# Six levels of row counts instead of four for the experts of a fused attention, dense and routed MLP kernel

## The chip, the cores and the metric

The kernel runs on one core of one Trainium2 chip. The metric is the device time of one launch in microseconds (us). TensorE (PE), VectorE (DVE), ScalarE (ACT), GpSimd (POOL) and SyncE (SP) each work through their own instructions in order; SP issues nearly all DMAs.

## The reference, cut to what matters

Attention over 2 batches, 8 heads and 576 positions gives 1152 tokens of 512 features. A dense layer with the activation `h * cos(h)` follows, and then a routed layer of 8 experts:

```python
def _moe2_ref(x, w_gate, w1, w2, capacity):      # x 1152 x 512, w1 8 x 512 x 1024, w2 8 x 1024 x 512
    expert_idx = np.argmax(x @ w_gate, axis=1)
    ...
    for i in range(N):                            # each token goes to one expert, up to capacity 288
        e = expert_idx[i]
        if counts[e] < capacity:
            disp[e, counts[e]] = x[i]
    ...
    h = np.maximum(np.einsum('ecd,edf->ecf', disp, w1), 0.0)
    y = np.einsum('ecf,efd->ecd', h, w2)
    ...
            out[i] = gate_w[i] * y[expert_idx[i], pos[i]]
```

How many tokens an expert gets depends on the inputs. Counted with the reference on its default draw, experts 0 to 7 get 206, 162, 138, 155, 108, 127, 112 and 144.

## The kernel before, in words

One core does everything in stages: attention (to about 100 us), the first dense matmul (to 200 us), the second dense matmul with the routing (to 309 us), and the experts (from 295 us to the end). Every product is done in three fp16 matmuls (high by high, high by low, low by high), so each weight that comes from DRAM in float32 is split in two on the chip.

**Rows of an expert.** The tokens are scattered by expert into a DRAM buffer `disp` with room for 288 rows an expert. A matmul needs a row count that is fixed in the program, but the counts are known only at run time. So the kernel holds several whole programs for the experts, one for each line of a table SIZES (a level), and takes the first level whose eight row counts are all large enough; a general program with 288 rows each stands behind them. The choice is made in `counts()`: `limit` holds the counts of all levels (filled by POOL memsets of one element in `consts2`, L172), one DVE comparison a level is made (L1201), and a sum over them gives the number of levels that are too small. Every engine then branches on that number (`arms`, L1351).

**Which expert is which.** The two experts expected to be largest (expert 0, and one chosen after five of nine token tiles) have their first 144 rows worked ahead of the branch. The columns of SIZES are then: what those two have left over (columns 1 and 2), the whole of the third chosen expert (column 3), and the other five in order of size (columns 4 to 8). Below they are called experts A to H by column. With the counts above they need 62, 14, 162, 144, 138, 127, 112 and 108 rows.

**One expert of `ns` rows** (`expert`, L1032). Its rows come by a transposing DMA into `eX` (ns rounded up to 16 rows, L1011). Layer 1 is eight blocks of 128 hidden features, each 12 matmuls of `ns` columns into one PSUM bank (L1042), evicted by ACT (the high half, with ReLU, L1044) and DVE (the low half, L1045) into `eH`. Layer 2 has two forms:

```python
    def flipped(ns):
        return ns <= 112 or 128 < ns <= 224
```

Flipped: four blocks of 24 matmuls with `ns` columns (L1064), four evictions (L1066), eight transposes for more than 128 rows or four for fewer (L1071), then one or two scaled stores (L1050). Not flipped: 24 matmuls of 512 columns for each 128 rows (L1081), and the store. The stores go to POOL, which scatters the rows to the output (L1051); padding rows are dropped there.

**The weights.** An expert has eight loads of 512 KB (four of w1, four of w2), each into one of four staging tiles `ws` (SP, L967 and L971), which ACT (high half, L656) and DVE (low half, L657) split; then the tile is free for the next load. The pairs of buffers `win`, `gall`, `gall`, `wout` take the experts in turn: D and H use `wout`, E `win`, F and G `gall`. At the branch 40 loads are still to be split, those of D to H. They are numbered 1 to 40 here: 1 to 8 are D's, 25 to 28 G's w1, 29 to 32 G's w2, 33 to 36 H's w1, 37 to 40 H's w2.

**The order.** Within a level the work of an expert and the next are interleaved by `adv(e, k)`, which takes expert e up to its step k (LA is 4, LB is 4):

```python
        for e in range(n):
            ...
            adv(e, KE)                 # rest of layer 1
            state["l1"] = e + 1
            adv(e + 1, la)             # next expert: four blocks of layer 1
            ...
            adv(e, KE + l2s[e])        # layer 2
            adv(e + 1, lb)
            adv(e, KE + l2s[e] + 1)    # transposes, stores
```

How many splits are put between these steps is set by a credit that grows with the matmul columns written so far (in `adv`: `12 * ns` for a block of layer 1, `12 * cols` for a step of layer 2), and the scheduler of the framework then settles the order in which each engine's instructions stand. PSUM has six banks for this, `ps_s`, `ps_pt` and `ps_mm` with two each, taken in turn.

Of the kernel before, what the change touches and what calls it, by code (L numbers as in the profile page):

```python
# [39 lines left out]
NST = 1  # L40
HALF = 1
SIZES = (
# [4 lines left out]
)  # L47
WP = 8
XR = 4
# [1333 lines left out]
```

## Time and profile before

| | |
|---|---|
| time, median of 3 runs | 434.71 us (433.16 to 439.06) |
| the profiled execution's own time | 437.53 us |
| its span from first to last instruction | 435.8 us |
| share of the span busy: PE, DVE, ACT, POOL | 92%, 72%, 63%, 34% |
| mean clock of TensorE granted | 0.98 of full speed |
| first matmul behind the branch | 328.61 us |
| last matmul ends, last store of rows issued | 429.0, 430.05 us |

The profile is one execution on the chip. Times are microseconds from the start of the span, durations of an instruction count from its start to its end, and a busy PE is not PE at its peak, since matmuls overlap: what a row of matmuls costs is read from the start of the next one. "[2.59 <-DVE eH L1045]" behind a row is idle time ahead of it and what ended it. L12 is line 12 of the kernel before; in the kernel after, every line from the table on is two lines further down.

### The profile page before, as it was taken

The numbers are of one execution on the slowest core, as the hardware profiler recorded it, in microseconds if no ns is written. First come the engines' busy times: TensorE is split into PE (matmuls) and PEld (weight loads), VectorE is DVE, ScalarE is ACT, GpSimd is POOL, SyncE is SP. The second block draws the span as 40 slices with busy tenths as digits, with TensorE's granted clock in tenths as the row PEclk, the third lists the DMA queues.
The fourth block names the chain that finished last, engine by engine and source line by source line (L and its number), as shares of the span: only waits on it lengthen the run. The fifth ranks groups of instructions, "written<-read, shape, count | busy, mean of one in ns | idle before, by whom it ended". The sixth has DMA issues, their size and how long they took to land.

```text
span 435.8 us, 10790 instructions
## 1 busy us (share of the span) xinstructions
PE 401.6 (92%) x4008; PEld 291.5 (67%) x4008; DVE 312.6 (72%) x767; ACT 275.6 (63%) x634; POOL 150.0 (34%) x242
## 2 busy tenths in 40 slices
PE   2799999999999999989999999797999999798893
PEld 1588888886666666544444454355988999798862
DVE  7769999749998499989875665654824576667570
ACT  6679989977888577775234433525536667677560
POOL 7668888553454345445000032010011012022030
PEclk9989999999999999999999999899999999899898
DMA  7979995103389933312567476758697689888741
GB/s 164 206 169 195 165 214 142 52 2 99 97 231 304 335 121 99 96 57 90 193 186 236 111 160 225 221 127 252 206 213 159 178 277 251 312 280 278 250 133 39
DMA packets 91228, 77.61 MB, mean 178 GB/s; under 512 B 64006, under 2 KB 72198, under 8 KB 91167
## 3 DMA queue, kind: packets, MB, share of 16 engines
q1 hardware_dynamic: 87855, 71.85, 60.2%
q0 software_dynamic: 2256, 4.73, 3.2%
q8 instruction: 33, 0.54, 0.6%
q10 hardware_dynamic: 1056, 0.26, 0.3%
q14 instruction: 28, 0.23, 0.2%
HBM read 57.66 MB, written 12.36 MB: 161 GB/s over the span
## 4 chain that ended last, share of the span: by engine, by line
PE 30%; DMA 11%; DVE 7%; ACT 5%; issue 5%; SPq 2%; POOL 1%; POOLq 0%; ACTq 0%; DVEq 0%
DMA ws<-in_moe_w_dram 9%; PE ps_mm L865 6%; PE ps_sm L865 4%; PE ps_mm L1064 3%; PE ps_s L1042 2%; PE ps_pt L865 2%; PE ps_s L865 2%; PE ps_pt L1042 2%; PE ps_pt L1064 2%; PE ps_mm L1042 2%; PE ps_s L1064 2%; DVE gall L657 2%; ACT gall L656 2%; DMA xr<-row 1%; DVE ws L679 1%
## 5 line engine op out<-in xcount | busy, mean ns | idle before, releaser
L810 PEld LDWEIGHTS <-win 128*128 128x128 f16 x576 | 56.2, 98 | 37.9 <-issue 1.1
L865 PEld LDWEIGHTS <-gall 128*128 128x128 f16 x432 | 41.3, 99 | 50.5 <-issue 4.0
L865 PE MATMUL ps_mm<-wout,gall 128*128 128x512 f16 x240 | 57.9, 387 | 1.3 <-DVE n__2934 L824 1.3
L1051 POOL DMA_INDIRECT out_dram<-gall,eM x16 | 20.2, 1266 | 101.8 <-ACT gall L1050 94.1
L657 DVE SCALAR_TENSOR_TENSOR gall<-ws,gall 128x1024 f16<-128x1024 f32 x32 | 38.7, 1220 | 23.0 <-ACT gall L656 22.6
L656 ACT ACTIVATE gall<-ws 128x1024 f16<-128x1024 f32 x32 | 33.6, 1058 | 26.9 <-DMA ws<-in_moe_w_dram 26.8
L656 ACT ACTIVATE wout<-ws 128x512 f16<-128x512 f32 (+1 forms) x32 | 27.2, 860 | 27.7 <-DVE ws L679 20.3
L239 ACT ACTIVATE z<-z,st 128x256 f32<-128x256 f32 (+4 forms) x72 | 41.9, 587 | 0.8 <-DVE st L239 0.8
L239 DVE CUSTOM_DVE_ANT_0 z<-ps_s,zm 128x512 f32<-128x512 f32 (+3 forms) x72 | 34.5, 510 | 10.2 <-PE ps_s L242 9.0
L945 POOL DMA_INDIRECT disp<-row,rsli x9 | 9.2, 1020 | 93.9 <-ACT rm L926 48.6
L657 DVE SCALAR_TENSOR_TENSOR wout<-ws,wout 128x512 f16<-128x512 f32 (+1 forms) x32 | 30.3, 954 | 10.7 <-ACT wout L656 10.6
L810 PE MATMUL ps_s<-xT,win 128*128 128x384 f16 x192 | 34.1, 326 | 0.0
L810 PE MATMUL ps_pt<-xT,win 128*128 128x384 f16 x192 | 33.8, 326 | 0.0
L810 PE MATMUL ps_mm<-xT,win 128*128 128x384 f16 x192 | 33.8, 326 | 0.0
L245 PE MATMUL ps_pt<-idf,z 128*128 128x128 f32 x192 | 30.2, 282 | 1.3 <-DVE p L239 1.3
L823 ACT ACTIVATE y<-y,quarter 128x384 f32<-128x384 f32 x48 | 29.2, 609 | 0.1
L239 ACT COPY p<-ps_pt 128x512 f32<-128x512 f32 (+2 forms) x48 | 25.2, 525 | 6.0 <-PE ps_pt L245 5.7
L657 DVE SCALAR_TENSOR_TENSOR win<-ws,win 128x1024 f16<-128x1024 f32 x16 | 19.5, 1224 | 12.4 <-ACT win L656 12.1
L1042 PEld LDWEIGHTS <-gall 128*128 128x128 f16 x480 | 27.9, 97 | 0.7 <-DVE gall L657 0.6
L245 PEld LDWEIGHTS ps_pt<-idf,z 128*128 128x128 f32 x192 | 23.1, 145 | 6.3 <-issue 1.5
L1064 PEld LDWEIGHTS <-gall 128*128 128x128 f16 x384 | 23.9, 101 | 2.8 <-issue 2.8
L242 PE MATMUL ps_s<-kT,qT 128*128 128x384 f16 (+7 forms) x128 | 24.1, 307 | 1.0 <-DMA kT<-bt 0.5
(497 smaller groups left out, 897.2 us busy)
## 6 DMA issues: line engine op xcount, KB each, us to landing
ws<-in_moe_w_dram SPq DMA_DIRECT2D x64, 512.0 KB, 5.3
ws<-in_moe_w_in_dram SPq DMA_DIRECT2D x16, 512.0 KB, 5.3
ws<-in_moe_w_out_dram SPq DMA_DIRECT2D x16, 512.0 KB, 4.0
disp<-zc SPq DMA_DIRECT2D x18, 257.0 KB, 7.2
out_dram<-zc SPq DMA_DIRECT2D x9, 256.0 KB, 4.7
qf<-in_q_dram SPq DMA_DIRECT2D x16, 128.0 KB
vf<-in_v_dram SPq DMA_DIRECT2D x16, 128.0 KB, 2.9
kf<-in_k_dram SPq DMA_DIRECT2D x14, 128.0 KB, 3.5
```

The source lines that it names most:

```text
L239: return pin(f(*a, **kw))
L242: return pin(nc.tensor.matmul(out_, **kw))
L245: return pin(nc.tensor.transpose(out_, in_, id_))
L656: nc.scalar.activation(hi, src, AF.Copy, scale=sc)
L657: (eng or nc.vector).scalar_tensor_tensor(lo, src, sc, hi, ALU.mult, ALU.subtract)
L810: nc.tensor.matmul(hp[:, 0:CH], lhsT=win[a][:, kk, fs], rhs=xT[:, x_, kk, xs], start=(n == 0), stop=(n == 3 * KD - 1))
L823: nc.scalar.activation(y, y, AF.Sin, scale=TWO_PI, bias=quarter)
L865: gate["pe"] = nc.tensor.matmul(xp, lhsT=G[c][:, a, f, ts], rhs=wout[w_][:, f, :], start=(f == 0 and n == 0), stop=(f == KF - 1 and n == 2))
L945: sc = nc.gpsimd.indirect_dma_start(out=disp, out_offset=bass.IndirectOffsetOnAxis(ap=sli.bitcast(U32), axis=0), in_=r, in_offset=None, bo ...
L1042: gate["pe"] = nc.tensor.matmul(hp[:, 0:ns], lhsT=a1[:, kk, a, fs], rhs=X[:, x_ * KD + kk, 0:ns], start=(n == 0), stop=(n == 3 * KD - 1))
L1051: sc = nc.gpsimd.indirect_dma_start(out=out, out_offset=bass.IndirectOffsetOnAxis(ap=M[:, b, 1:2].bitcast(U32), axis=0), in_=y, in_offset= ...
L1064: nc.tensor.matmul(yp[:, 0:ns], lhsT=a2[:, f, w_, d * 128:(d + 1) * 128], rhs=Hh[:, a, f, :], start=(n == 0), stop=(n == 3 * KE - 1))
```

## The change

The table gets six lines instead of four. Nothing else is edited.

```diff
 SIZES = (
-    (64, 56, 184, 168, 152, 144, 128, 120),
-    (72, 64, 192, 168, 152, 144, 136, 128),
-    (88, 88, 200, 176, 160, 152, 136, 128),
-    (128, 96, 216, 192, 176, 152, 144, 144),
+    (64, 48, 176, 160, 152, 128, 128, 120),
+    (64, 48, 176, 168, 160, 144, 128, 128),
+    (64, 64, 184, 176, 168, 144, 128, 128),
+    (64, 64, 184, 176, 168, 152, 144, 128),
+    (72, 64, 200, 184, 168, 152, 144, 128),
+    (72, 80, 224, 184, 176, 160, 144, 128),
 )
```

The first line loses 8 rows in columns B, C and D and 16 in F, 40 of 1016 in all. By `flipped`, F's 144 rows were the flipped form and its 128 rows are not. The most that columns A and B can hold falls from 128 and 96 to 72 and 80, and the two transposing DMAs issued for them ahead of the branch fall to 80 rows each. The `limit` table has 60 elements instead of 40, and `counts()` makes six comparisons instead of four. Ahead of the branch the instructions of every engine stand in the same order as before but for these; within the first level the scheduler's order moves.

On ACT, around the split of H's first weights (`wout_95<-ws`, loads 33 to 36; `wout_96<-ws` is w2). Before:

```order
L1044 ACTIVATE eH<-ps_mm 128x128
L656 ACTIVATE wout_95<-ws_91 128x1024
L1066 COPY xq<-ps_s 128x144
L1066 COPY xq<-ps_pt 128x144
L656 ACTIVATE wout_95<-ws_92 128x1024
L1066 COPY xq<-ps_mm 128x144
L1066 COPY xq<-ps_s 128x144
L1044 ACTIVATE eH<-ps_pt 128x128
L1044 ACTIVATE eH<-ps_mm 128x128
L1044 ACTIVATE eH<-ps_s 128x128
L656 ACTIVATE wout_95<-ws_4070 128x1024
L1044 ACTIVATE eH<-ps_pt 128x128
```

After, the same stretch, from F's one store on:

```order
L1052 ACTIVATE gall<-ps_s,eM_3450 128x512
L1046 ACTIVATE eH<-ps_pt 128x128
L1046 ACTIVATE eH<-ps_mm 128x128
L1046 ACTIVATE eH<-ps_s 128x128
L1046 ACTIVATE eH<-ps_pt 128x128
L658 ACTIVATE wout_95<-ws_91 128x1024
L658 ACTIVATE wout_95<-ws_92 128x1024
L658 ACTIVATE wout_95<-ws_4090 128x1024
L658 ACTIVATE wout_95<-ws_90 128x1024
L658 ACTIVATE wout_96<-ws_91 128x2x512
L1046 ACTIVATE eH<-ps_mm 128x120
```

The four evictions of F's flipped layer 2 (`xq`) are gone, and the five splits that stood between evictions now stand together behind G's last evictions.

On DVE, at the end of the level, the low halves of H's last weights (`wout_96<-ws`, loads 38 to 40) and of its layer 1 (`eH`). Before, from load 39 on:

```order
L657 SCALAR_TENSOR_TENSOR wout_96<-ws_4070,wout_96 128x2x512
L1045 SCALAR_TENSOR_TENSOR eH<-ps_mm,eH 128x120
L1045 SCALAR_TENSOR_TENSOR eH<-ps_s,eH 128x120
L1045 SCALAR_TENSOR_TENSOR eH<-ps_pt,eH 128x120
L657 SCALAR_TENSOR_TENSOR wout_96<-ws_90,wout_96 128x2x512
L1045 SCALAR_TENSOR_TENSOR eH<-ps_s,eH 128x120
L1045 SCALAR_TENSOR_TENSOR eH<-ps_pt,eH 128x120
L1045 SCALAR_TENSOR_TENSOR eH<-ps_mm,eH 128x120
L1045 SCALAR_TENSOR_TENSOR eH<-ps_s,eH 128x120
```

After, from load 38 on:

```order
L659 SCALAR_TENSOR_TENSOR wout_96<-ws_92,wout_96 128x2x512
L1047 SCALAR_TENSOR_TENSOR eH<-ps_pt,eH 128x120
L1047 SCALAR_TENSOR_TENSOR eH<-ps_mm,eH 128x120
L659 SCALAR_TENSOR_TENSOR wout_96<-ws_4090,wout_96 128x2x512
L1047 SCALAR_TENSOR_TENSOR eH<-ps_pt,eH 128x120
L659 SCALAR_TENSOR_TENSOR wout_96<-ws_90,wout_96 128x2x512
L1047 SCALAR_TENSOR_TENSOR eH<-ps_mm,eH 128x120
L1047 SCALAR_TENSOR_TENSOR eH<-ps_s,eH 128x120
L1047 SCALAR_TENSOR_TENSOR eH<-ps_pt,eH 128x120
```

The last split had four of H's evictions behind it and has three; the fourth has moved ahead of it.

On ACT, the split of load 28, the last of G's w1, stood ahead of E's two stores and stands behind them.

On PE the order moves too. Before, when H's first four blocks of layer 1 are done, 2 of the 24 matmuls of G's layer 2 have gone by and 22 follow; after, 9 have gone by and 15 follow, and the blocks are cut in five pieces, by the weight load that each piece needs. The first four blocks of F and of G are cut in the same way.

## Rows read from the trace of the kernel before

**Rows 1.** Page, slices of 10.9 us: busy tenths of PE and of the DMA engines.

```profile
PE   2799999999999999989999999797999999798893
...
DMA  7979995103389933312567476758697689888741
```

**Rows 2.** Timeline of PE, from the branch on: start us, us, engine, line, form, count.

```profile
331.43 0.47 PE L1042 MATMUL ps_s<-eX,gall 128*128 128x56 f16 x12
331.74 0.47 PE L1042 MATMUL ps_pt<-eX,gall 128*128 128x56 f16 x12
...
338.38 1.11 PE L1042 MATMUL ps_mm<-eX,gall 128*128 128x184 f16 x12
339.33 1.11 PE L1042 MATMUL ps_s<-eX,gall 128*128 128x184 f16 x12
...
372.78 2.61 PE L1064 MATMUL ps_pt<-eH,wout 128*128 128x168 f16 x24 [2.59 <-DVE eH L1045]
...
398.73 1.66 PE L1064 MATMUL ps_s<-eH,gall 128*128 128x144 f16 x24
400.23 1.66 PE L1064 MATMUL ps_pt<-eH,gall 128*128 128x144 f16 x24
404.54 3.04 PE L1064 MATMUL ps_mm<-eH,gall 128*128 128x144 f16 x24 [2.64 <-DVE eH L1045]
...
411.15 0.83 PE L1042 MATMUL ps_pt<-eX,gall 128*128 128x128 f16 x12
411.82 0.60 PE L1071 MATMUL ps_mm<-idf,xq 128*72 128x128 f32 x4
...
416.36 4.91 PE L1081 MATMUL ps_mm<-gall,eH 128*128 128x512 f16 x22
421.11 0.79 PE L1042 MATMUL ps_s<-eX,wout 128*128 128x120 f16 x12
...
423.63 5.35 PE L1081 MATMUL ps_pt<-wout,eH 128*120 128x512 f16 x24
```

**Rows 3.** Windows of 5 us: PE, PEld, DVE, ACT, POOL busy, clock, DMA share, GB/s.

```profile
348.00:353.00 5.00, 5.00 (x70) 5.00 (x68) 4.55 (x7) 4.07 (x8) 1.20 (x1) 1.00 0.92 254
...
403.00:408.00 5.00, 3.46 (x30) 3.46 (x30) 3.15 (x6) 1.98 (x8) 0.00 (x0) 0.66 0.83 288
```

**Rows 4.** The staging tiles `ws` from 296 us on, by operation (min/median/max ns).

```profile
L656 ACT ACTIVATE gall<-ws x24: 1048/1057/1087, 297.6 to 402.0; 128x1024 f16<-128x1024 f32 x24
L657 DVE SCALAR_TENSOR_TENSOR gall<-ws,gall x24: 1203/1224/1226, 298.7 to 403.1; 128x1024 f16<-128x1024 f32 x24
...
DMA to landing us min/median/max: 5.2/5.7/6.6
```

**Rows 5.** Timeline of DVE, splits of weights: load 28, load 36 with the next two.

```profile
395.38 1.21 DVE L657 SCALAR_TENSOR_TENSOR gall<-ws,gall 128x1024 f16<-128x1024 f32 x1
...
414.86 3.50 DVE L657 SCALAR_TENSOR_TENSOR wout<-ws,wout 128x1024 f16<-128x1024 f32 x3 [0.83 <-ACT wout L656]
```

**Rows 6.** Timeline of ACT: the first of E's two stores; loads 36 to 38; load 40.

```profile
396.37 0.69 ACT L1050 ACTIVATE gall<-ps_s,eM 76x512 f32<-76x512 f32 x1
...
413.77 2.95 ACT L656 ACTIVATE wout<-ws 128x1024 f16<-128x1024 f32 x3
...
420.85 1.06 ACT L656 ACTIVATE wout<-ws 128x1024 f16<-128x1024 f32 x1 [1.65 <-DMA ws<-in_moe_w_dram]
```

**Rows 7.** Timeline of SP: the issue of load 36.

```profile
404.31 0.34 SPq L967 DMA_DIRECT2D ws<-in_moe_w_dram  x1
```

**Rows 8.** The lines that fill and compare the table of limits.

```profile
L172 POOL MEMSET limit<- x40: 88/88/137, 88.3 to 89.6; 1x1 f32 x40
...
L1201 DVE TENSOR_TENSOR ov<-ky,limit x4: 148/150/151, 309.1 to 309.3; 1x10 f32<-1x10 f32 x4
```

**Rows 9.** Timelines of POOL and DVE: the idle time behind the memsets and the comparisons.

```profile
92.19 0.61 POOL L239 COPY rsb<-rs 128x512 f32<-128x512 f32 x1 [1.90 <-DVE rs L239]
...
311.39 0.31 DVE L1045 SCALAR_TENSOR_TENSOR eH<-ps_mm,eH 128x144 f16<-128x144 f32 x1 [1.89 <-ACT eH L1044]
```

## The prediction

> **What bounds the kernel now.** I read the slices of the page first: PE shows a 9 nearly everywhere, and dips only in the last seven slices, where the DMA engines show 6 to 9 [rows 1]. Those slices are the experts, the only stage whose instructions the change moves, so the rest of the reading is there. The timeline of PE comes next. Behind the branch PE works gaplessly at first: 12 matmuls of 56 columns take 0.31 us from start to start, 12 of 184 take 0.95. Later it stops twice for some 2.6 us, at 372.78 and at 404.54, both times inside a flipped layer 2 [rows 2]. A window over the second stop shows the clock at 0.66 on the mean of 5 us, so part of it at the lower of its two levels, 1.2 GHz: the 24 matmuls behind the stop take 3.04 us, those of 400.23 1.66 [rows 2, 3]. So PE is the busiest engine, but it no longer sets the pace.
>
> What does is the stream of weights. A load needs 0.34 us to be issued, 5.7 to land, 1.06 on ACT and 1.22 on DVE [rows 4, 7]; only then is its tile free. That is 8.32 us a round for four tiles, 2.08 us a load if nobody is late. The DMA engines are 0.92 busy in the quiet window and 0.83 in the one with the stop [rows 3]. Before, load 28 (the last of G's w1) is split at 395.38 + 1.21 = 396.59 and load 36 (the last of H's w1) at 414.86 + 1.22 = 416.08 [rows 5]: 19.5 us for eight loads, 2.44 each, so 2.9 us above the rounds. Load 36 shows why: issued at 404.31, it should land by 410.0, but ACT splits it at 413.77 [rows 6, 7]. It stood behind evictions and stores of F and G that waited for the late PE.
>
> From load 36 on PE runs to the end: the rest of H's first blocks, 22 matmuls of G's layer 2 from 416.36, 48 of H's second blocks from 421.11, 24 of H's layer 2 from 423.63 to 428.98 [rows 2]. That is 12.9 us behind load 36. What follows (a store, a scatter, the drain) is untouched.
>
> **The change part by part.**
>
> *PE's work.* Eight columns fewer cost (0.95 - 0.31) / 16 = 0.04 us less for 12 matmuls [rows 2]. B, C and D each have 16 such groups: 0.64 us each, 1.9 together. F saves 0.64 in layer 1 (eight groups, sixteen columns fewer); its layer 2 goes from 4 x 1.50 us and 0.87 of transposes (411.82 to 412.69, the next work) to 24 matmuls of 512 columns at (421.11 - 416.36) / 22 = 0.216 us, 5.2 us [rows 2]. That is 1.7 less, so 2.3 in F and 4.2 us in all.
>
> For B the nearest rows are the 56-column ones, 25.8 ns a matmul [rows 2]. The Trainium skill (TensorE: Matmul & The Clock Gate, section "Wait — 56ns, not 53.3ns?") says that starts never follow each other by less than about 25 ns, however few the columns. By the 0.04 us B saves 0.64 us, by the rule 192 x 0.8 ns = 0.15; PE's sum would be 3.7 instead of 4.2. No row here is narrower and back to back.
>
> *What of it lies on the path.* Little of it directly: B to D are done long before PE waits for weights. What counts is when load 28 is split, how fast eight more follow, and what PE still has to do then.
>
> Load 28: in the new order of ACT it stands behind E's two stores, where it stood ahead of them. A store holds ACT for up to 0.69 us [rows 6]. Against that PE comes to these places up to 4.2 us earlier. The bounds are 1.4 us late and 4.2 us early; I take 1.0 late, 397.6, since loads 17 to 28 come by rounds of the tiles that an earlier PE doesn't shorten.
>
> Loads 29 to 36: F's four evictions and PE's stop at 404.54 are gone. After load 28 PE needs 20 matmuls of 512 columns (4.3 us) and G's four last blocks (0.67 each, 2.7 [rows 2]), so G's last evictions are ready at about 404.8 instead of 411.8. By rounds load 33 is only landing then, so the five splits that now stand together find their way free and run by rounds: 397.6 + 8 x 2.08 = 414.2, 1.9 earlier than before. The other ends are 2.44 us a load as before (417.1) and, with the shortest landing of 5.2 us, 1.96 a load (413.3) [rows 4].
>
> Behind load 36 there are now 4 small matmuls (0.2), 15 of G's layer 2 instead of 22 (3.2), H's 48 (2.5) and H's 24 (5.35 with the last one's end): 11.3 us instead of 12.9. End: 414.2 + 11.3 = 425.5 instead of 428.98.
>
> Two more things must be ready. Load 40 would be split at 414.2 + 4 x 2.08 = 422.5; H's layer 2 starts at 420.2 and wants it for its last six matmuls at 424.1. And three of H's evictions stand behind that split on DVE, at about 422.8 to 423.3; the first is wanted at 423.4. So the cover there is 0.6 us: if load 40 is later than that, the end is its split plus 2.4 us.
>
> *The table itself.* Twenty memsets more on POOL: the forty take from 88.3 to 89.6, so some 0.7 us, beside 1.90 us in which POOL waits for DVE behind them [rows 8, 9]. Two more comparisons: 0.15 us each at most, ahead of an instruction for which DVE waits 1.89 us for ACT [rows 8, 9]. Both zero; 0.7 and 0.3 us if the cover were gone. The smaller transposing DMAs ahead of the branch free queue time on SP where PE waits for none of them: zero. The two added levels are code that is branched over once, as two of the four were; no row bounds what their length costs, and I take zero.
>
> *Sum.* 428.98 becomes 425.5, 3.4 us less in the profiled execution: 437.53 to 434.1. That execution lies 2.8 us above the median of the runs, so I take the 3.4 us off the median: 434.71 - 3.4 = 431.3 us.
>
> **The rivals.**
>
> *The stream goes faster still.* If load 28 isn't late (396.6) and loads land in 5.2 us, load 36 is split at 412.3 and the end is 423.6: 5.4 us less, 429.3. If loads never held PE, G's last blocks would end at 403.8 and PE would need 2.5 + 5.2 + 2.5 + 5.35 us more: 419.4, 9.6 less, 425.1. For it: the DMA engines are not full. Against it: four tiles.
> The Trainium skill (HBM Reference, section "Specifications (TRN2)") gives a core that streams alone about 425 GB/s; as an estimate from that page, a 512 KB load would take 1.23 us, and this case would be the result. The trace has 254 and 288 GB/s in the two windows, and disagrees so far [rows 3].
>
> *The stream is DMA's own pace and nothing is gained there.* At 2.44 us a load from 397.6, load 36 is split at 417.1 and the end is 428.4: 0.6 less, 434.1. For it: a DMA share of 0.8 to 0.9 leaves little to win [rows 3]. Against it: load 36 demonstrably lay waiting.
>
> *Slower: PE waits at H's cuts and its clock falls.* The new order cuts the first blocks of F, G and H by weight loads that come 2.08 us apart or more, with about 1 us of PE work between. Before, a stop of 2.6 us was followed by the lower clock, which cost 3.04 - 1.66 = 1.4 us in the next block alone [rows 2, 3]. If the loads of H also come at 2.44 us, the waits fall in front of the last 11.3 us, and two blocks' worth of low clock make 428.4 + 2.8 = 431.2: 2.2 slower, 436.9. It decides from load 36 at about 414.9 (428.98 - 11.3 - 2.8), with a clock below 1.00 behind it. Against it: PE's short waits elsewhere show no lower clock.
>
> *The change doesn't do what it says.* F's count is 127 by the reference, one below the new limit of 128 (112 for G and 108 for H are far off). If the chip routes two tokens otherwise, a later level is taken, of 1016 or more rows, with F at 144 again: no gain, about 434.7. The trace before shows widths of the first level only, so it can't tell.
>
> **How the numbers follow.** Forecast, 429.7 to 433: 0.42. Faster stream, 426 to 429.7: 0.18. No gain, 433 to 435: 0.22. Slower by the clock, 435 to 438.5: 0.13. Another level: 0.05. The range from 427.0 to 436.0 leaves out some 0.06 below and 0.09 above, and holds the runs' own scatter. A difference of 2% is 8.7 us, about what a measurement of this kernel can tell from no change. Faster than 426.0 needs nearly the whole of PE's bound: 0.05. Slower than 443.4 has no mechanism here: 0.02. Within: 0.93.
>
> **What would show it.** Right: F's layer 2 as 24 matmuls at 0.216 us and no stop of 2.6 us inside a flipped layer 2 of F; G's last block over by about 405; load 36 split at about 414, and 11.3 us from there to the last matmul's end. Wrong: load 36 at 416 or later (the stream didn't gain), PE windows behind it at a clock below 1.00, or more than 2.4 us from load 40 to the end. Widths of 168, 160 and 144 in D, E and F would show another level.

## The result, and the profile after

| | before | after |
|---|---|---|
| median in this comparison | 437.46 us (6 runs) | 430.81 us (6 runs, 427.17 to 433.34) |
| ratio, 95% interval | | 0.9892 [0.9848, 0.9937] |
| the same kernel compared again | 435.03 us (30 runs) | 430.89 us (8 runs), 0.9907 [0.9874, 0.9941] |
| profiled execution, its span | 437.53, 435.8 us | 430.29, 428.2 us |

By these ratios the change is faster by 4.7 us in the first comparison (interval 2.8 to 6.6) and by 4.0 in the second (2.6 to 5.5); 3.4 was predicted. The ratio is not that of the two medians, which differ by 6.6 and 4.1 us. The slices of the page, 10.7 us each, that answer to [rows 1]:

```profile
PE   2799999999999999999999999797998999999783
...
PEclk9989999999999999999999999899999999999998
DMA  7979795203369932323667456947759298998851
```

The dips of PE in the experts' part are fewer now. The DMA engines hardly differ there. One window from the first matmul behind the branch to the end of the last one says more. First the kernel before (its columns: from:to, length, then PE, PEld, DVE, ACT and POOL busy with their instructions, clock, DMA share, GB/s):

```profile
328.61:428.98 100.37, 94.07 (x1432) 87.78 (x1432) 63.50 (x107) 64.80 (x137) 17.32 (x13) 0.97 0.76 230
```

and the kernel after:

```profile
325.00:421.47 96.47, 88.72 (x1352) 77.83 (x1352) 62.69 (x106) 63.58 (x133) 15.84 (x12) 1.00 0.75 239
```

The window is 3.9 us shorter: PE works 5.4 us less and idles 1.4 us more (7.75 instead of 6.30). Of the 5.4 us some 3 are the lower clock in that one trace of before: in a trace of it with the clock at 1.00 throughout, the control below, PE works 91.1 us. The other 3.6 us between the two traces lie ahead of the branch, where nearly nothing changed; in a second trace of the changed kernel its first matmul stands at 331.22, so this is scatter, and times are counted from the branch from here on. The timeline of PE after (start us, us, engine, line, form, count, idle time ahead):

```profile
329.41 0.46 PE L1044 MATMUL ps_s<-eX,gall 128*128 128x48 f16 x12
329.71 0.46 PE L1044 MATMUL ps_pt<-eX,gall 128*128 128x48 f16 x12
...
392.89 4.48 PE L1083 MATMUL ps_s<-gall,eH 128*128 128x512 f16 x20
397.20 0.83 PE L1044 MATMUL ps_pt<-eX,gall 128*128 128x128 f16 x12
397.88 0.83 PE L1044 MATMUL ps_mm<-eX,gall 128*128 128x128 f16 x12
400.32 0.83 PE L1044 MATMUL ps_s<-eX,gall 128*128 128x128 f16 x12 [1.61 <-DVE eH L1047]
400.99 0.83 PE L1044 MATMUL ps_pt<-eX,gall 128*128 128x128 f16 x12
403.14 0.28 PE L1044 MATMUL ps_mm<-eX,wout 128*128 128x120 f16 x2 [1.31 <-ACT wout L658]
...
408.89 0.28 PE L1044 MATMUL ps_mm<-eX,wout 128*128 128x120 f16 x2 [2.00 <-ACT wout L658]
...
410.37 3.40 PE L1083 MATMUL ps_s<-gall,eH 128*128 128x512 f16 x15
413.61 0.79 PE L1044 MATMUL ps_pt<-eX,wout 128*128 128x120 f16 x12
...
416.13 5.34 PE L1083 MATMUL ps_mm<-wout,eH 128*120 128x512 f16 x24
```

The widths of 48 and the unflipped layer 2 of F show that the first level was taken. F's matmuls follow each other at (397.20 - 392.89) / 20 = 0.2155 us. The stops of 2.6 us inside flipped layer 2 [rows 2] are gone. Shorter ones stand in G's last blocks and where H's first blocks are cut, and the clock stays at its upper level there. The window over the longest, which answers to [rows 3]:

```profile
405.00:410.00 5.00, 2.90 (x34) 1.64 (x31) 2.74 (x3) 1.99 (x2) 0.00 (x0) 1.00 1.01 358
```

The stream around load 36, on DVE, on ACT and on SP, which answers to [rows 5 to 7]. DVE, load 32 and loads 36 and 37:

```profile
400.58 1.22 DVE L659 SCALAR_TENSOR_TENSOR gall<-ws,gall 128x1024 f16<-128x1024 f32 x1
...
408.87 2.50 DVE L659 SCALAR_TENSOR_TENSOR wout<-ws,wout 128x1024 f16<-128x1024 f32 x2 [2.26 <-ACT wout L658]
```

ACT, load 36:

```profile
407.78 1.06 ACT L658 ACTIVATE wout<-ws 128x1024 f16<-128x1024 f32 x1 [2.81 <-DMA ws<-in_moe_w_dram]
```

SP, the issue of load 36:

```profile
401.82 0.35 SPq L969 DMA_DIRECT2D ws<-in_moe_w_dram  x1
```

Load 32 frees its tile at 400.58 + 1.22 = 401.80. Load 36 is issued into it at 401.82, ACT waits for its landing, and it is split at 408.87 + 1.23 = 410.10. That is a round of 8.30 us. In the second trace of the change (its first matmul behind the branch at 331.22) the same round, from load 32 to load 36, takes 414.16 - 406.83 = 7.33 us:

```profile
405.61 1.22 DVE L659 SCALAR_TENSOR_TENSOR gall<-ws,gall 128x1024 f16<-128x1024 f32 x1 [1.55 <-ACT gall L658]
...
412.93 1.23 DVE L659 SCALAR_TENSOR_TENSOR wout<-ws,wout 128x1024 f16<-128x1024 f32 x1 [1.64 <-ACT wout L658]
```

Before, load 36 lay waiting for ACT; now ACT waits for it. The loads just ahead of it still lie: 33 to 35 stand in one row on ACT without a wait for a landing, behind G's last evictions:

```profile
402.03 2.94 ACT L658 ACTIVATE wout<-ws 128x1024 f16<-128x1024 f32 x3
```

### The profile page after: what moved, and what is told of

It reads as the page before. It is cut to its first block, busy times and chain, and to the rows that moved or that the text cites. A ratio compares the mean times of both kernels' runs of the same rounds, so it can differ in the third digit from the quotient of the medians.

```text
span 428.2 us, 10640 instructions
## 1 busy us (share of the span) xinstructions
PE 395.1 (92%) x3928; PEld 281.6 (66%) x3928; DVE 311.8 (73%) x768; ACT 274.8 (64%) x630; POOL 149.2 (35%) x261
## 4 chain that ended last, share of the span: by engine, by line
PE 32%; DMA 9%; DVE 7%; issue 5%; ACT 4%; SPq 2%; POOL 1%; POOLq 0%; ACTq 0%; DVEq 0%
DMA ws<-in_moe_w_dram 8%; PE ps_mm L867 7%; PE ps_sm L867 5%; PE ps_pt L1044 3%; PE ps_s L1066 3%; PE ps_mm L1044 2%; PE ps_s L867 2%; PE ps_pt L867 2%; PE ps_s L1044 2%; PE ps_pt L1066 2%; PE ps_mm L1066 2%; DVE gall L659 1%; ACT gall L658 1%; DVE y L818 1%; SPq L1013 1%
## 5 line engine op out<-in xcount | busy, mean ns | idle before, releaser
L867 PEld LDWEIGHTS <-gall 128*128 128x128 f16 x432 | 41.3, 98 | 49.3 <-issue 2.5
L1053 POOL DMA_INDIRECT out_dram<-gall,eM x15 | 18.8, 1252 | 98.4 <-ACT gall L1052 77.4
L1044 PEld LDWEIGHTS <-gall 128*128 128x128 f16 x480 | 27.0, 97 | 3.7 <-issue 1.9
L658 ACT ACTIVATE win<-ws 128x1024 f16<-128x1024 f32 x16 | 16.8, 1055 | 10.9 <-DMA ws<-in_moe_w_dram 10.9
```

The source lines that it names most:

```text
L658: nc.scalar.activation(hi, src, AF.Copy, scale=sc)
L867: gate["pe"] = nc.tensor.matmul(xp, lhsT=G[c][:, a, f, ts], rhs=wout[w_][:, f, :], start=(f == 0 and n == 0), stop=(f == KF - 1 and n == 2))
L1044: gate["pe"] = nc.tensor.matmul(hp[:, 0:ns], lhsT=a1[:, kk, a, fs], rhs=X[:, x_ * KD + kk, 0:ns], start=(n == 0), stop=(n == 3 * KD - 1))
L1053: sc = nc.gpsimd.indirect_dma_start(out=out, out_offset=bass.IndirectOffsetOnAxis(ap=M[:, b, 1:2].bitcast(U32), axis=0), in_=y, in_offset= ...
```

## The experiments

All runs in one table. Ratio is to the kernel before on the same chip. The rest is from one trace each: time from the first matmul behind the branch to the end of the last, PE busy and idle in it, and the end of the splits of loads 28, 36 and 40, counted from that first matmul.

| kernel | ratio [95%] | window | PE busy | idle | 28, 36, 40 |
|---|---|---|---|---|---|
| before | | 100.4 | 94.1 | 6.3 | 68.0, 87.5, 94.6 |
| before again | 1.0027 [0.9989, 1.0066] | 97.5 | 91.1 | 6.4 | 67.2, 84.6, 91.8 |
| levels alone | 0.9989 [0.9955, 1.0023] | 99.1 | 92.7 | 6.5 | 67.2, 86.2, 94.0 |
| F alone | 0.9928 [0.9891, 0.9966] | 94.0 | 88.9 | 5.1 | 66.9, 82.8, 91.2 |
| B, C, D alone | 0.9921 [0.9886, 0.9957] | 96.1 | 90.6 | 5.5 | 68.0, 84.2, 93.0 |
| B alone | 1.0033 [0.9999, 1.0067] | 99.5 | 91.2 | 8.3 | 70.0, 87.2, 94.5 |
| order of B, C, D cut; old widths | 1.0004 [0.9973, 1.0035] | 99.2 | 92.6 | 6.6 | 70.8, 87.4, 96.3 |
| B, C, D cut; old order | 0.9960 [0.9924, 0.9996] | 99.7 | 92.7 | 7.0 | 67.3, 86.8, 93.9 |
| the change | 0.9892 [0.9848, 0.9937] | 96.5 | 88.7 | 7.8 | 67.6, 85.1, 91.9 |
| the change again | 0.9907 [0.9874, 0.9941] | 94.3 | 88.6 | 5.8 | 67.1, 82.9, 89.8 |
| before, five tiles | 0.9930 [0.9899, 0.9960] | 96.4 | 92.0 | 4.4 | 67.5, 83.5, 88.1 |
| the change, five tiles | 0.9950 [0.9916, 0.9984] | 94.7 | 88.3 | 6.5 | 69.1, 83.3, 90.0 |
| the change, old credit | 0.9924 [0.9887, 0.9961] | 94.7 | 88.9 | 5.7 | 64.9, 80.5, 88.2 |
| the change, old credit, five tiles | 0.9804 [0.9739, 0.9870] | 90.0 | 87.0 | 3.1 | 61.5, 76.1, 82.6 |

**The levels and a control.** Levels alone: lines 2 to 6 of the new table behind the first line of before. Control: the kernel before, unchanged.

```diff
     (64, 56, 184, 168, 152, 144, 128, 120),
-    (72, 64, 192, 168, 152, 144, 136, 128),
...
+    (64, 48, 176, 168, 160, 144, 128, 128),
...
```

> Six levels: the first line of before, the other five of the change. So the 20 memsets, the two comparisons, the 80-row transposing DMAs ahead of the branch and the longer program are there, and the first level is that of before. Theories 1 and 2: a ratio of 1.000 within 0.003, 100.4 us behind the branch. If the smaller transposing DMAs or anything else ahead of the branch were worth something, the first matmul behind the branch would start earlier than in the control kernel of the same call by more than the kernels of before differ among themselves.

> The kernel before itself, unchanged, as a control: a ratio of 1.00; all theories expect about 100.4 us behind the branch (99.9 to 100.9). What is open is how far the start of the first matmul behind the branch scatters: 328.6 us in the one profile of before, 325.0 in that of the change, where the stages ahead of it are the same but for 20 memsets and the size of two DMAs. If it is scatter, this profile can lie anywhere between 324 and 330.

Neither differs from the kernel before. So twenty memsets, two comparisons and two more levels cost nothing that can be measured (the interval runs from 2.0 us gained to 1.0 lost), and the gain is put down to the first line. The first three rows of the table have the same widths, and their single traces scatter by 2.9 us in the window and in load 36, nearly as much as the gain. On their mean, 99.0 and 86.1, against the two traces of the change, 95.4 and 84.0, the window is 3.6 us shorter.

**F alone, and B, C, D alone.**

```diff
-    (64, 56, 184, 168, 152, 144, 128, 120),
+    (64, 56, 184, 168, 152, 128, 128, 120),
```

> The table of before, but its first line has 128 rows instead of 144 for F; B, C, D keep 56, 184, 168, and there are four levels. Measured from the first matmul behind the branch to the end of the last one, before has 100.4 us and the whole change 96.5. Theory 1 (the form of F's layer 2: its four evictions and PE's stop inside it go, the weights of H are split sooner; the 8 columns of B, C, D are worth nothing): 96.5 to 97.5, a ratio of 0.990 to 0.994. Theory 2 (every matmul column taken out of PE shortens the end alike, 2.3 of 4.2 us in F): 98.1, a ratio of 0.995. Theory 3 (nothing in the experts matters, the gain is scatter ahead of the branch): 100.4 and a ratio of 1.00.

```diff
-    (64, 56, 184, 168, 152, 144, 128, 120),
+    (64, 48, 176, 160, 152, 144, 128, 120),
```

> The table of before, but its first line has 48, 176 and 160 rows for B, C and D; F keeps 144 rows in the flipped form, and there are four levels. Theory 1: PE reaches F some 1.4 to 1.9 us earlier and waits there for weights; from the branch to the last matmul's end 99.4 to 100.4 us instead of 100.4, a ratio of 0.997 to 1.000, and a stop of PE inside F's layer 2 as before. Theory 2: 98.5 us, a ratio of 0.995 to 0.996. Theory 3: 100.4. B's blocks of 12 matmuls with 48 columns: 0.30 us from start to start by the change's trace, not 0.27.

F alone gives 0.0072 x 436.4 = 3.1 us, B to D alone 3.4 us. Theory 1 falls: B to D carry as much as F. Theory 2 had 0.995 for both, which the intervals still hold. PE's busy time falls by 2.2 us for F against the control, as its columns say, and by 0.6 for B to D. Busy time holds the run-out of the last matmul ahead of every stop (a row of 12 with 128 columns lasts 0.83 us, and the next starts after 0.67), so with more and shorter stops it tells less than what was saved. Idle time falls by 0.9 for B to D. These two traces show 1.4 of the 3.4 us; the rest is within the scatter of traces.

**B alone.**

```diff
-    (64, 56, 184, 168, 152, 144, 128, 120),
+    (64, 48, 184, 168, 152, 144, 128, 120),
```

> The table of before with 48 instead of 56 rows for B in its first line, nothing else. By the trace of the change 12 matmuls of 48 columns take 0.303 us against 0.31 for 56, so PE saves 0.1 us in all; but the scheduler's order moves nearly as for B, C and D together (five of G's 24 matmuls of 512 columns stand ahead of H's last piece instead of two, and an eviction or two change places with splits). If columns make the gain: a ratio of 0.999 to 1.000. If the order makes it: 0.992 to 0.997, and fewer or shorter stops of PE in the flipped layer 2 of D, E and F than the control's 1.84, 1.26 and 1.88 us.

No gain. The order at the level's end moves the same way as with B to D, though not as far: 12.3 us follow load 36, where it was 12.9 before and 11.8 with B to D. So this speaks against that part of the order as the cause; the next kernel, with the whole order of B to D, settles it.

**Widths against order.** The credit counts matmul columns, 0.55 of a load for 2400 of them. B to D have 4608 columns fewer, so their cut puts the splits 1.06 loads later in the order, besides saving PE time. Two kernels part these. In the first the widths are old and the order is new:

```diff
-                ns = plan[e][1]
+                ns = {56: 48, 184: 176, 168: 160}.get(plan[e][1], plan[e][1]) if group == "out0" else plan[e][1]
```

> All widths are those of the kernel before (B 56, C 184, D 168, F 144); only the credit that places the splits counts B, C and D 8 columns narrower, so each engine's instructions stand in the order of the run with B, C and D cut. Columns theory (the narrower matmuls gave that run its 0.992): no gain here, ratio 0.998 to 1.003, and PE stops 1.4 to 2.6 us in D's layer 2 as before. Order theory (splits of loads 16 to 19 one place later between D's evictions take that stop away): ratio 0.991 to 0.995, no stop over 0.7 us in D's layer 2, PE busy behind the branch still about 91.1 us, PE idle there 5.5 instead of 6.4 us or less.

In the second the widths are 48, 176 and 160, and the dictionary is turned round, so the order is old:

> The converse: the widths of the run with B, C and D cut (48, 176, 160), with a credit that counts them at their old widths, so the order is that of the kernel before. Columns theory: ratio 0.990 to 0.995, PE busy behind the branch about 90.5 us. Order theory: the stop of 1.4 to 2.6 us in D's layer 2 is back and eats what PE saves, ratio 0.997 to 1.001. If both parts give half, this run and the other stand near 0.996 each.

The order alone gives nothing: its splits simply come later (load 28 at 70.8). The widths alone give 0.4%, 1.7 us with an interval from 0.2 to 3.3; their columns save 1.4 (0.64 us each for C and D, 0.1 for B). Together they gave 0.8%; the intervals overlap, so whether the order adds something to the narrower widths stays open. What becomes of PE's saving in the old order is seen in the timeline of PE of the second kernel:

```profile
373.53 3.10 PE L1064 MATMUL ps_pt<-eH,wout 128*128 128x160 f16 x24 [3.12 <-DVE eH L1045]
...
404.37 2.89 PE L1064 MATMUL ps_mm<-eH,gall 128*128 128x144 f16 x24 [2.52 <-DVE eH L1045]
```

The stop in D's layer 2 ends 373.53 - 329.13 = 44.4 us behind the branch; before it was 372.78 - 328.61 = 44.2 [rows 2], in the control 44.6. PE came earlier and waited longer, 3.12 us instead of 2.59, for an eviction that DVE makes behind splits. Here the stream sets the time, and the columns saved ahead of it are lost in this place. The window over the stop in the kernel before shows the DMA engines full, which neither window of [rows 3] does:

```profile
368.50:373.50 5.00, 2.41 (x34) 2.27 (x32) 3.34 (x6) 2.52 (x7) 0.00 (x0) 1.00 1.05 389
```

So what the widths alone gained can't be these columns whole, and where it comes from stays open. In the order of B to D cut with their narrow widths that stop does not occur.

**Five tiles, first try.** NST counts the staging tiles beyond the first three. The fifth is paid for by two levels and smaller buffers of rows and of layer 1 (`eX`, `eH`); the same edit in the kernel before (first text) and in the change (second):

```diff
-NST = 1
+NST = 2
...
-        eb["X"] = pool.tile([128, XR * 2 * KD * 224], F16, name="eX")
+        eb["X"] = pool.tile([128, XR * 2 * KD * 192], F16, name="eX")
...
```

> The kernel before with the same fifth staging tile (its table cut to the first two lines, buffers to 192 rows; the first level is that of before). If the tiles set the pace: a ratio of 0.980 to 0.990, and the split of load 36 at 82 to 84 us behind the branch instead of 84.6 to 87.5. If not: 0.997 to 1.003. PE's matmul columns are those of before, so whatever this gains is not gained by columns.

> The change with a fifth staging tile for the weights (NST 2); to make room the table keeps its first four lines only and the buffers of an expert are cut from 224 to 192 rows, which the first level doesn't notice. If the four tiles set the pace of the loads (8.32 us a round by the trace before), a round of five gives 1.66 us a load unless the DMA engines are full first: load 36 comes 3 to 5 us earlier, the end behind the branch falls from 96.5 to 92 to 94 us, a ratio to before of 0.975 to 0.985. If the loads run at the DMA engines' own pace, or if the end is bound by PE's columns, a ratio like the change's own, 0.987 to 0.993.

> The change itself again: the first comparison gave 0.9892 with an interval from 0.985 to 0.994, F's column alone 0.9928, those of B, C and D alone 0.9921. If the two parts add up, 0.985; if they share one gain, 0.989 to 0.992. Its profile also shows whether the branch at 325.0 us (327.6 to 329.7 in all other kernels) belongs to the change or to that one execution: all theories expect 327 to 330 here.

The kernel before gains 0.7% with every column as it was, so its ring of four did hold it. The stop in D's layer 2 is gone, as it should be if the stream made it:

```profile
371.12 1.90 PE L1062 MATMUL ps_s<-eH,wout 128*128 128x168 f16 x24
372.86 1.90 PE L1062 MATMUL ps_pt<-eH,wout 128*128 128x168 f16 x24
```

The change gains nothing by the fifth tile (0.9950 beside 0.9907 for itself), which the ring alone doesn't explain. On ACT in the change with five tiles, loads 33 to 36 stand in one row without any wait for a landing; they had landed and stood behind evictions:

```profile
402.10 1.06 ACT L656 ACTIVATE gall<-ws 128x1024 f16<-128x1024 f32 x1 [1.93 <-DMA ws<-in_moe_w_dram]
...
407.05 3.88 ACT L656 ACTIVATE wout<-ws 128x1024 f16<-128x1024 f32 x4
```

**The old credit.** F's unflipped layer 2 counts 6144 columns instead of 13,824, and layer 1 1536 fewer, 2.1 loads of credit; with B to D the change holds the splits back by 3.2 loads. The last two kernels have the widths of the change and count all experts as before, with four tiles and with five:

```diff
-                ns = plan[e][1]
-                cols = 512 * blocks(ns)[0] if not flipped(ns) else 2 * ns
+                ns = (64, 56, 184, 168, 152, 144, 128, 120)[e] if group == "out0" else plan[e][1]
+                cols = 512 * blocks(ns)[0] if not flipped(ns) else 8 * ns if group == "out0" and e == 5 else 2 * ns
```

> Widths of the change, four tiles, the same early credit: the splits stand as in the kernel before. If every column that PE saves is a gain whatever the order: PE busy about 88.6 us, ratio 0.988 to 0.993, as the change. If the stream sets the ends of the stops: PE stops for about 3 us in D's layer 2 until some 44 us behind the branch, load 36 is split at 86 us or later, and the ratio is 0.993 to 0.998.

> Widths of the change, five staging tiles, and a credit that counts all experts at the widths of the kernel before, F's flipped layer 2 included: the splits stand as early as in the run of the kernel before with five tiles. If late splits were what kept five tiles from helping the change (order and tiles must suit each other): PE busy about 88.5 us behind the branch, stops of 2 to 3 us in all, 91 to 92 us to the last matmul, ratio 0.982 to 0.988, faster than the change itself. If the narrower widths leave nothing for a fifth tile to win: 94 to 95 us and a ratio of 0.989 to 0.994, as the change and its run with five tiles had.

With four tiles the early order is worth no more than the late one (0.9924 and 0.9907). So the change's gain comes with its widths and F's form, and not with the order that they brought along. Each theory is half right there: D's stop is back, until 372.78 - 329.64 = 43.1 us behind the branch, as the stream theory says,

```profile
372.78 1.82 PE L1066 MATMUL ps_pt<-eH,wout 128*128 128x160 f16 x24 [2.88 <-DVE eH L1047]
```

but load 36 comes at 80.5, far ahead of the 86 that it gave, and the ratio is the change's. With five tiles the early order is worth 1.5% (0.9804 beside 0.9950): by the ratio 8.5 us less than the kernel before on that chip (medians 427.71 and 435.47 us) and the fastest version of this study. It rests on few runs, and the mean granted clock of these was 0.992 beside 0.986, which by the scatter of all runs (last section) goes with about 1 us. Its window, and the stretch in which the weights stream:

```profile
328.90:418.94 90.04, 86.99 (x1352) 77.96 (x1351) 63.01 (x106) 63.35 (x133) 15.35 (x12) 1.00 0.80 252
...
360.00:405.00 45.00, 43.28 (x607) 39.49 (x604) 35.96 (x54) 36.39 (x69) 10.35 (x7) 1.00 0.99 329
```

The same 45 us in the change with five tiles:

```profile
360.00:405.00 45.00, 41.71 (x559) 37.27 (x557) 31.43 (x47) 32.59 (x63) 9.51 (x7) 1.00 0.87 281
```

The DMA engines went from 0.87 to 0.99 busy: the early order keeps the five tiles filled, the late one leaves landed loads lying. On ACT the splits of loads 34 and 36 to 39 now wait for a landing instead of lying behind evictions; loads 36 and 37:

```profile
402.71 1.06 ACT L656 ACTIVATE wout<-ws 128x1024 f16<-128x1024 f32 x1 [1.34 <-DMA ws<-in_moe_w_dram]
404.52 1.06 ACT L656 ACTIVATE wout<-ws 128x1024 f16<-128x1024 f32 x1 [0.75 <-DMA ws<-in_moe_w_dram]
```

Of PE's idle time 3.05 us are left in its window. This version has only four levels, and the most rows that it holds before the general program are fewer than in either kernel; on other draws of the inputs it would take a later level or that program sooner.

## Why the prediction was right, and where not

- **Load 36: right, and its reason.** Predicted 414.2, or 85.6 us behind the branch; the two traces have 85.1 and 82.9, before 87.5 and 84.6. On the means above it came 2.1 us earlier; 1.9 was predicted. It no longer waits behind evictions. That all five splits find their way free was not so: load 33, issued at 393.76, was taken by ACT only at 402.03, behind G's.
- **The round of four tiles: 0.34 us too long.** The 5.7 us to land count from the start of the issue, as the prediction itself has them where load 36, issued at 404.31, lands by 410.0. So the round holds the issue twice. It is 5.7 + 1.06 + 1.22 = 7.98 us, 2.00 a load, and the sum then gives load 36 at 413.6 and a gain of 4.1 us instead of 3.4. The rounds measured from load 32 to load 36, 8.30 and 7.33, lie to both sides; that the first is so near 8.32 is luck. Eight loads behind load 28 took 410.10 - 392.60 = 17.5 us, 2.19 each (2.08 predicted, 2.44 before), and 15.8 in the second trace.
- **The tail: right.** 421.47 - 410.10 = 11.4 us behind load 36; 11.3 predicted, 12.9 before. Load 40 came 6.8 us behind load 36 and not 8.3, so the cover of 0.6 us was not touched.
- **G's last blocks: the number right, by luck.** The next work after them could start at 400.99 + 0.67 = 401.66, 76.7 us behind the branch; 404.8, or 76.2, was predicted. But load 28 came 1.4 us sooner than forecast, and a stop of 1.61 us in these blocks that I had not seen took that back. In the second trace, without that stop, it is 74.4.
- **F's form: right.** 2.3 us predicted, 2.2 less PE time measured with F alone.
- **B's floor: the page was right.** Twelve matmuls of 48 columns start 0.303 us apart, 25.3 ns each, where the columns alone would give 0.27. B saves (0.31 - 0.303) x 16 = 0.1 us. The 0.15 that follows from the Trainium skill (TensorE: Matmul & The Clock Gate, section "Wait — 56ns, not 53.3ns?") stands, not the 0.64 of the rows; B alone gained nothing.
- **Load 28, 1.0 us late: mis-sized.** It was split 67.6 and 67.1 us behind the branch, not 69.0, and not later than before (68.0 and 67.2). So it came 1.4 us and more ahead of the forecast; in the first trace the eight loads behind it gave 0.9 of that back (17.5 us instead of 16.64), in the second nothing. This term and the round both point to a gain above the 3.4 us forecast. Both intervals of the measured gain hold 3.4, so whether it did come out higher is not shown.
- **"Little of it directly: B to D are done long before PE waits for weights": wrong.** B to D alone gave 3.4 us, their widths without the order 1.7. The trace of before had a stop in D's layer 2 [rows 2], and I read it as the stream's. It is: in the old order it ends at 43 to 45 us behind the branch whatever PE saves. Even so B to D gained; which part of it came from columns behind that stop, and which from the order that goes with narrower widths, these runs don't part.
- **The base: partly luck.** The sum starts from a trace of before with the lower clock behind two stops. Its window was 100.4 us; the control has 97.5, and its load 36, at 84.6, lies ahead of the forecast. The forecast of 431.3 lies 0.5 from the 430.81 measured, but it was taken off a median of 434.71, and the kernel before had 437.46 in this comparison.
- **What the prediction didn't see.** The credit counts columns, so a cut of columns puts the splits later, 3.2 loads here. I compared the orders and priced two places; that the change makes landed loads lie longer was not asked. With four tiles it costs nothing measurable, with five 1.5%.
- **The rivals.** The fall of the clock at H's cuts did not come in the two traces of the change: stops of 1.31 and 2.00 us, in the second trace 2.05 and 1.38, and a clock of 1.00 in the window over the 2.00. It did come in the trace with the old credit and four tiles (last section). The level taken was the first. "No gain" is excluded by both intervals. The faster stream is what the last version shows: 85.1 became 76.1 for load 36. The DMA engines moved 329 GB/s at 0.99 busy over 45 us, 358 at 1.01 over 5 us, and in the kernel before 389 at 1.05; the 425 GB/s of the Trainium skill (HBM Reference, section "Specifications (TRN2)") are not reached in these windows.

The parts don't add: 3.1 and 3.4 us alone, 4.0 to 4.7 together. Each of the parts has about 1.6 us to either side, so a sum of 6.5 has some 2.2 and is not excluded. PE's idle time says that some is given back: 7.8 and 5.8 us in the change, 5.1 and 5.5 in its parts. How much, these runs don't settle.

## What to carry to other kernels

Where an order is written by a budget that counts work (here columns for loads), a cut of the work moves the order as well: compare the place of each transfer's use before and after, and try the new sizes with the old budget. Columns saved ahead of a wait that the stream ends are lost at that wait. That columns saved behind the last such wait are gained whole is likely and not shown: F's 2.2 us of PE time gave 3.1, with an interval from 1.5 to 4.8. One more buffer helps only if the order asks for the data early enough to fill it: here the fifth tile and the early order together took the change from 0.990 to 0.980, and neither gained it anything without the other.

## What the runs showed of the hardware

A stop is not always followed by the lower clock, and its length alone doesn't decide: behind stops of 2.59, 2.64 [rows 2], 3.12 and 2.52 us the next block ran slow (3.10 us instead of 1.82 in the second order run), and so did two blocks behind one of 2.18 in the run with the levels alone,

```profile
402.23 2.38 PE L1066 MATMUL ps_mm<-eH,gall 128*128 128x144 f16 x24 [2.18 <-DVE eH L1047]
404.40 2.62 PE L1066 MATMUL ps_s<-eH,gall 128*128 128x144 f16 x24
```

where 1.66 is the usual time [rows 2]. But it did not behind 2.88 us in the change with the old credit, where the next block took 1.82. In that same trace the clock fell later, behind three stops of 0.38 to 0.98 us at H's cuts:

```profile
405.55 0.28 PE L1044 MATMUL ps_mm<-eX,wout 128*128 128x120 f16 x2 [0.55 <-ACT wout L658]
406.81 0.23 PE L1044 MATMUL ps_mm<-eX,wout 128*128 128x120 f16 x1 [0.98 <-DVE wout L659]
...
407.57 0.28 PE L1044 MATMUL ps_mm<-eX,wout 128*128 128x120 f16 x2 [0.38 <-ACT wout L658]
```

The window behind them:

```profile
408.00:412.00 4.00, 4.00 (x39) 3.13 (x36) 3.31 (x4) 1.77 (x3) 0.00 (x0) 0.57 0.90 269
```

The scatter of the runs goes with the clock: within the runs of a kernel, 0.01 less of the mean granted clock of an execution goes with about 2 us more, and that accounts for about a third of the scatter. In the second comparison the mean over the runs was 0.987 for the kernel before and 0.986 for the change, so its 4.0 us are not the clock's.

In 11 of the 14 traces PE stops 2 to 8 us behind the first matmul behind the branch for 0.4 to 2.6 us, in one or two places, where the profile names no releaser ("issue"). With the longest the clock fell; the window over it, from the kernel before with five tiles:

```profile
333.00:338.00 5.00, 2.41 (x49) 2.32 (x45) 1.23 (x1) 0.46 (x3) 0.00 (x0) 0.73 0.73 86
```

The longest of these stops is more than half of the differences looked for here, which is why ratios over many runs decide and single traces don't.
